# The query features on GpSimd, with wide products and a new order of steps

## The chip, the cores and the metric

The kernel runs on one core of a Trainium2 chip. The metric is the device time of one execution in microseconds. A core has five engines that run beside each other and wait for one another through semaphores: TensorE (PE, matrix products; PEld is its loading of weights), VectorE (DVE), ScalarE (ACT), GpSimd (POOL) and SyncE (SP), which here only issues transfers (DMA).

## The reference, cut to what matters

```python
def phi(x):                                  # x: [4, 4, 1088, 32]
    a = einsum('rd,bhsd->bhsr', S1, x)       # r = 8
    b = einsum('rd,bhsd->bhsr', S2, x)
    return einsum('bhsi,bhsj->bhsij', a, b)  # 64 features
kv  = einsum('bhsf,bhsd->bhfd', phi(k), v);  z = phi(k).sum(axis=2)
x   = (phi(q) @ kv) / (phi(q) @ z + 1e-6)    # 4352 tokens x 128
h   = x @ w_in                               # 4352 x 2048
P   = a0 + a1*h + a2*h**2 + a3*h**3
Q   = 1 + |b0|*|h| + |b1|*h**2
out = (P / (Q + 1e-6)) @ w_out
```

First comes a linear attention whose features are products of two sketches, then a layer with a rational function in the middle.

## The kernel before, in words

**Two halves that run at once.** The attention works by batch: `Keys` (lines 236 to 314) makes the sums over keys and values, `Queries` and `Spread` (lines 317 to 433) make x for blocks of queries and put it, transposed, into `xT`. The layer works by units: a unit is 4096 columns of (a stretch of features) x (a stretch of tokens), 17 in all, numbered 0 to 16 (lines 436 to 446). Units 1 to 14 have 512 tokens and 8 blocks of features; units 0, 15 and 16 have 256 tokens and all 16 blocks. A unit has two halves of 2048 columns; the second half of unit 16 is cut in two again (`QUARTER`).

**One unit.** PE makes h in four parts of 1024 columns (`hidden`, L455), ACT copies each into `hh` in bf16 (`evac`, L461). DVE makes u = |h| (L484), w = |b1| u + |b0| (L490) and w u (L495), for a whole unit at once or, for units in `SPLIT_A`, by halves. ACT makes r = 1/Q by a logarithm and an exponential (L546, L550), by halves. Then DVE makes s = h r (L554), and the third term in one of two ways. Normally p = a3 h + a2 comes from ACT or DVE (`P_ON_ACT` says which, half by half; L541, L536), m is g = h s (L558), x is g = g p (L569), and PE adds up r, s and g with three scaled copies of w_out (`gather`, L588). For the halves in `HORNER`, m is g = h p, then DVE adds a1 to g (step v, L564), x is g = g s, and PE adds up r and g alone: the s products fall away (L577). `WIDE_S`, `WIDE_M`, `WIDE_X` and `WIDE_P` name the units in which s, m, x or p is one instruction of 4096 columns instead of two of 2048 (`skip`, L518); for m and x both halves must be Horner or both not. r, s, g and p lie in rings (L497): four halves each for r, s and g, two for p.

**One block of queries.** The last ten blocks are `Spread`: PE makes the sketches (L409), ACT copies them to SBUF (L415), SP writes them to DRAM and reads them back spread out, as `a_all` and `b_all` (L420 to L428, one buffer each); then the features are their product (`features`, L432: 128 x 768 or 128 x 640 in f32), both factors in SBUF. PE multiplies the features with the sums of the keys (L365), ACT and DVE divide (L376, L380, L385), PE transposes (L391), ACT copies into `xT` (L398). The first three blocks (`Queries`) make their features from a factor in PSUM (L354, L357).

**The order.** `ORDER` (lines 21 to 57) is a list written out by hand: each entry is a step and its unit, block or batch, and every engine gets its instructions in that order. h0 to h3 and e0 to e3 are `hidden` and `evac`, u, w, y, ln, ex, pa (p on ACT), pd (p on DVE), s, m, v, x the steps above (0 and 1 behind a letter are the halves), G0 to G8 the parts of `gather`; qt, qs, qc, qf, qp, qd, qi, qx, qb, qk are the steps of a query block, qf its features, qp the product that reads them; kt to kk those of the keys; lk, lq, lv, lw, lx load; wo scales w_out; ba takes |b|; st writes out; tn:0 and tn:4 give PE 11 and 2 idle products (`TURNS`, L170) into an otherwise unused bank.

Of the kernel before, what the change touches and what calls it, by code (L numbers as in the profile page):

```python
# [26 lines left out]
ex0:0 u1:1 h2:2 qf:3 w1:1 qc:4 e1:2 qp:3 e2:2 s0:0 pa0:0 h3:2 y1:1 h0:2 qd:3 wo:5 e3:2 qi:3 m0:0 G0:0 e0:2 qx:3 G1:0
ln0:1 kt1:2 x0:0 qb:3 ks0:2 u1:2 qk:3 G2:0 ex0:1 lk:3 pd0:1 G3:0 w1:2 G4:0 pa1:1 kp1:1 y1:2 kc0:2 ln1:1 G5:0 qf:4 lv:2
qs:5 kf0:2 kk:1 ex1:1 qp:4 s0:1 ks1:2 qd:4 qc:5 qi:4 ln0:2 qt:7 G0:1 qx:4 m0:1 qb:4 G1:1 qk:4 s1:1 ex0:2 h3:3 x0:1
kc1:2 h2:3 m1:1 e3:3 kf1:2 h0:3 e2:3 kt1:3 ln1:2 s0:2 h1:3 st:0 m0:2 e0:3 qs:7 x1:1 e1:3 h2:4 ex1:2 u1:3 h3:4 pd1:2  # L30
pa0:2 w1:3 kp1:2 s1:2 e2:4 x0:2 e3:4 h0:4 lv:3 qf:5 pa0:3 y1:3 qp:5 qc:7 e0:4 h1:4 m1:2 qd:5 ln0:3 qi:5 qt:9 G2:1 qx:5
e1:4 x1:2 qb:5 G3:1 qk:5 u1:4 ex0:3 G4:1 m0:3 G5:1 pa1:3 G0:2 w1:4 h0:5 kt0:3 ln1:3 m1:3 h2:5 y1:4 kk:2 ex1:3 ks0:3
G1:2 e0:5 s1:3 G2:2 ln0:4 G3:2 h1:5 v0:3 ex0:4 qf:7 x0:3 G4:2 e2:5 qs:6 s0:4 qc:6 h3:5 e1:5 pd0:4 ln1:4 m0:4 h1:6 v1:3
e3:5 x0:4 pa1:4 h0:6 u1:5 qt:8 G5:2 e1:6 w1:5 ex1:4 h3:6 st:2 y1:5 e0:6 qp:7 e3:6 s1:4 G0:3 pa0:5 lq:3 G2:3 x1:3 qs:8
m1:4 h2:6 ln0:5 m0:5 G3:3 e2:6 x1:4 G5:3 ex0:5 qf:6 G0:4 u1:6 G1:4 qc:8 qd:7 ln1:5 qi:7 qp:6 w1:6 G2:4 qx:7 qd:6 pa0:6
qi:6 v0:5 qb:7 G3:4 qx:6 y1:6 qb:6 qk:7 G4:4 qk:6 ex1:5 h3:7 m0:6 pa1:5 G5:4 s1:5 h1:7 e3:7 st:4 h2:7 m1:5 e1:7 ln0:6
x0:5 h0:7 qt:10 x1:5 e2:7 G0:5 e0:7 qf:8 ks1:3 kc0:3 ex0:6 u1:7 qs:9 h1:8 v0:6 qc:9 w1:7 ln1:6 h3:8 s0:6 e1:8 pd1:6
qp:8 ex1:6 y1:7 h0:8 e3:8 s1:6 kc1:3 ln0:7 h2:8 x0:6 e0:8 m1:6 G2:5 qd:8 ex0:7 G3:5 qi:8 kf0:3 G4:5 kf1:3 G5:5 e2:8
qs:10 ln1:7 u1:8 kp1:3 qx:8 w1:8 ex1:7 qb:8 G0:6 qf:9 qk:8 y1:8 qc:10 h3:9 pa0:7 s0:7 h0:9 e3:9 s1:7 ln0:8 h2:9 qt:12
m0:7 e0:9 G0:7 x1:6 e2:9 h1:10 ex0:8 x0:7 qt:11 h1:9 u1:9 pa0:8 m1:7 G2:6 pd1:7 e1:9 G3:6 s0:8 e1:10 G4:6 u0:9 ln1:8  # L40
h3:10 w1:9 m0:8 qp:9 ex1:8 x1:7 h2:10 x0:8 qd:9 kk:3 e3:10 qi:9 w0:9 pa0:9 h0:10 qf:10 y0:9 qp:10 e2:10 y1:9 e0:10
G5:6 qx:9 qd:10 ln0:9 qi:10 qb:9 s1:8 G1:7 qx:10 G2:7 qk:9 u1:10 ex0:9 G3:7 m1:8 qb:10 G4:7 qk:10 s0:9 ln1:9 G5:7
qs:11 pd1:8 h1:11 w1:10 qc:11 ex1:9 x1:8 h0:11 e1:11 m0:9 pa1:9 h3:11 y1:10 e0:11 G0:8 s1:9 e3:11 h2:11 ln0:10 x0:9
h0:12 m1:9 e2:11 pd0:10 ex0:10 h1:12 u1:11 x1:9 e0:12 G1:8 w1:11 e1:12 G2:8 ln1:10 G3:8 s0:10 G4:8 y1:11 G5:8 ex1:10
qs:12 G0:9 m0:10 G1:9 ln0:11 h3:12 s1:10 ex0:11 x0:10 h2:12 qf:11 pa1:10 m1:10 G2:9 s0:11 G3:9 e3:12 G4:9 x1:10 qc:12
ln1:11 qp:11 pd0:11 m0:11 G5:9 qd:11 e2:12 G0:10 qi:11 x0:11 ex1:11 G1:10 u1:12 G2:10 pa1:11 qx:11 G3:10 w1:12 qb:11
G4:10 qk:11 s1:11 pa0:12 h1:13 y1:12 h3:13 e1:13 m1:11 ln0:12 h2:13 st:6 x1:11 ex0:12 G5:10 qf:12 G0:11 st:8 e3:13
qp:12 s0:12 e2:13 st:10 h0:13 ln1:12 m0:12 u1:13 h2:14 e0:13 x0:12 ex1:12 u0:13 h3:14 w1:13 w0:13 e2:14 y1:13 e3:14
h1:14 pa1:12 y0:13 h0:14 s1:12 qd:12 e1:14 qi:12 m1:12 G1:11 e0:14 qx:12 G2:11 ln1:13 u1:14 qb:12 G3:11 pd0:13 G4:11
ex1:13 w1:14 G5:11 x1:12 G0:12 qk:12 ln0:13 h0:15 s1:13 pd1:13 ex0:13 G1:12 y1:14 G2:12 e0:15 h2:15 s0:13 ln0:14 m1:13  # L50
h3:15 e2:15 m0:13 ex0:14 h1:15 x1:13 x0:13 e3:15 G3:12 s0:14 e1:15 h2:16 ln1:14 u1:15 G4:12 m0:14 ex1:14 G5:12 w1:15
# [17 lines left out]
@with_exitstack  # L69
def kernel(  # L70
    ctx: ExitStack,
# [164 lines left out]
    class Keys:  # L236
# [33 lines left out]
        def features(self, part):  # L270
            n = self.PARTS[part][1]
            k_p = self.k_p[part] = tmp.tile([128, 5, H, R, R], FP, name="k_p", bufs=3)
            nc.vector.tensor_mul(  # L273
                out=k_p[:, 0:n].rearrange("p t h i j -> p (t h) i j"),
                in0=self.ab[part][:, :, :, 0, :].rearrange("p t h r -> p (t h) r")[:, :, :, None]
                    .broadcast_to([128, n * H, R, R]),
                in1=self.sk[part][:, 0:n].rearrange("p t h r -> p (t h) r")[:, :, None, :]
                    .broadcast_to([128, n * H, R, R]))
# [123 lines left out]
    class Spread(Queries):  # L402
# [26 lines left out]

        def features(self):  # L430
            self.q_p = tmp.tile([128, 2, QW], FP, name="q_pT")
            nc.vector.tensor_mul(out=self.q_p[:, :, :self.n], in0=self.a[:, :2 * self.n].rearrange("p (c n) -> p c n", c=2),  # L432
                                 in1=self.bb[:, :2 * self.n].rearrange("p (c n) -> p c n", c=2))


# [52 lines left out]
    def d_w(i, c):
        t = mine(i, "w", mid, 2)
        nc.vector.tensor_scalar(out=t[:, c], in0=live[i]["u"][:, c], scalar1=ab1, scalar2=ab0, op0=AX.mult, op1=AX.add)  # L490

    @halves(SPLIT_A)
    def d_y(i, c):
        t = live[i]["w"]
        nc.vector.tensor_mul(out=t[:, c], in0=t[:, c], in1=live[i]["u"][:, c])  # L495
# [36 lines left out]

    @skip(WIDE_P, on_act)
    def d_p(i, h, hh):
        if not on_act(i, first(h)):
            nc.vector.tensor_scalar(out=part_of(i, "p", h), in0=hh, scalar1=a3, scalar2=a2, op0=AX.mult, op1=AX.add)  # L536
# [14 lines left out]

    @skip(WIDE_S)
    def d_s(i, h, hh):
        nc.vector.tensor_mul(out=part_of(i, "s", h), in0=hh, in1=part_of(i, "r", h))  # L554
# [163 lines left out]
```

## Time and profile before

| | |
|---|---|
| runs | 272.06, 272.32, 272.9 us, median 272.32 |
| span of the profiled execution | 270.8 us; its own time is given by no other number |
| PE, DVE, ACT, POOL busy | 257.7, 256.7, 248.8, 2.9 us |
| DVE instructions | 278 |
| DMA | 19.55 MB, mean 72 GB/s |

How to read it: a group of instructions has one line of the kernel, an engine, an operation, what it writes and reads with the shapes, and the count; then the busy time in us, the mean of one in ns, and the idle time ahead of them with what ended it. In a view by time a line begins with the start and the duration in us. Where instructions overlap, the busy time counts a moment once.

### The profile page before, as it was taken

Reading aid. Unit: us, or ns where it says so; the run is one execution under the profiler, and the core shown is the slowest. Engines: PE = TensorE matmul, PEld = TensorE weight load, DVE = VectorE, ACT = ScalarE, POOL = GpSimd, SP = SyncE. Lnnn points to the kernel's source line nnn. Section 1 sums busy time; section 2 is a strip of 40 time slices with the busy share of each in tenths; the row PEclk is TensorE's granted clock in tenths of the full one; section 3 lists DMA queues with packets and bytes.
Section 4 is the critical chain, followed back from the end, with each engine's and each line's share of the span. In section 5 each row is a group of like instructions: output and inputs, shape, how many; then the busy total and the mean of one; then the engine's idle time right before and its main releaser. Section 6 shows DMA issues by size and latency. Waiting matters only on the chain.

```text
span 270.8 us, 3732 instructions
## 1 busy us (share of the span) xinstructions
PE 257.7 (95%) x1382; PEld 147.5 (54%) x1397; DVE 256.7 (95%) x278; ACT 248.8 (92%) x224; POOL 2.9 (1%) x24
## 2 busy tenths in 40 slices
...
DVE  3777999999999999999999999999999999999994
ACT  1268999998999999999999999999999999999991
...
GB/s 167 265 323 151 156 38 136 117 90 96 76 106 34 12 118 100 77 75 33 97 6 123 7 0 3 119 11 0 15 97 73 43 0 0 2 39 1 0 2 79
DMA packets 30530, 19.55 MB, mean 72 GB/s; under 512 B 20400, under 2 KB 26672, under 8 KB 30512
## 3 DMA queue, kind: packets, MB, share of 16 engines
...
q8 instruction: 11, 0.18, 0.3%
...
## 4 chain that ended last, share of the span: by engine, by line
ACT 47%; PE 34%; issue 8%; DVE 5%; DMA 4%; SPq 0%; ACTq 0%; DVEq 0%
PE h_ps L455 16%; ACT ln L546 13%; ACT r L550 12%; ACT hh L461 12%; PE att_ps L588 10%; ACT p L541 7%; PE att_ps L365 3%; DMA v_sb<-in_v_dram 2%; PE att_ps L302 2%; DMA k_sb<-in_k_dram 2%; DVE g L558 2%; DVE s L554 1%; ACT xT L398 1%; PE att_ps L391 1%; PE att_ps L409 1%
## 5 line engine op out<-in xcount | busy, mean ns | idle before, releaser
L455 PE MATMUL h_ps<-xT,w_in_sb 128*128 128x512 f32 (+1 forms) x320 | 125.8, 537 | 2.8 <-ACT hh L461 1.9
L455 PEld LDWEIGHTS h_ps<-xT,w_in_sb 128*128 128x128 f32 x320 | 58.3, 190 | 55.2 <-issue 37.3
L461 ACT CAST hh<-h_ps 128x1024 bf16<-128x1024 f32 x68 | 67.5, 1027 | 3.5 <-PE h_ps L455 3.1
L588 PEld LDWEIGHTS <-w_out 128*128 128x128 bf16 x460 | 45.5, 100 | 45.9 <-issue 14.3
L546 ACT ACTIVATE ln<-w 128x2048 f32<-128x2048 bf16 (+1 forms) x35 | 66.0, 1887 | 0.7 <-DVE w L495 0.6
L550 ACT ACTIVATE r<-ln 128x2048 bf16<-128x2048 f32 (+1 forms) x35 | 65.8, 1880 | 0.6 <-PE att_ps L588 0.2
L541 ACT ACTIVATE p<-hh,a_sb 128x2048 bf16<-128x2048 bf16 (+1 forms) x23 | 46.7, 2035 | 0.1
L554 DVE TENSOR_TENSOR s<-hh,r 128x2048 bf16<-128x2048 bf16 (+2 forms) x33 | 41.0, 1246 | 0.2 <-ACT r L550 0.2
L495 DVE TENSOR_TENSOR w<-w,u 128x4096 bf16<-128x4096 bf16 (+2 forms) x22 | 39.4, 1798 | 0.1
L588 PE MATMUL att_ps<-g,w_out 128*128 128x512 bf16 (+1 forms) x154 | 34.8, 350 | 4.3 <-DVE g L569 3.9
L558 DVE TENSOR_TENSOR g<-hh,s 128x2048 bf16<-128x2048 bf16 (+1 forms) x30 | 35.2, 1175 | 0.0
L569 DVE TENSOR_TENSOR g<-g,p 128x2048 bf16<-128x2048 bf16 (+1 forms) x30 | 35.1, 1178 | 0.1
L588 PE MATMUL att_ps<-r,w_out 128*128 128x512 bf16 (+1 forms) x154 | 34.8, 353 | 0.3
L588 PE MATMUL att_ps<-s,w_out 128*128 128x512 bf16 (+1 forms) x137 | 29.3, 342 | 0.2
L490 DVE TENSOR_SCALAR w<-u,b_abs 128x4096 bf16<-128x4096 bf16 (+2 forms) x22 | 23.8, 1090 | 0.0
L484 DVE TENSOR_SCALAR u<-hh 128x4096 uint16<-128x4096 uint16 (+2 forms) x22 | 21.4, 976 | 1.6 <-ACT hh L461 1.5
L365 PEld LDWEIGHTS att_ps<-kvz,q_pT 128*128 128x128 f32 x144 | 17.7, 191 | 4.6 <-issue 2.0
L365 PE MATMUL att_ps<-kvz,q_pT 128*128 128x66 f32 x144 | 17.9, 273 | 0.1
L302 PEld LDWEIGHTS att_ps<-v_sb,k_p 128*64 128x64 f32 (+1 forms) x288 | 8.8, 138 | 1.9 <-DVE qT L325 0.8
L536 DVE TENSOR_SCALAR p<-hh,a_sb 128x2048 bf16<-128x2048 bf16 x12 | 9.7, 808 | 0.0
L302 PE MATMUL att_ps<-v_sb,k_p 128*64 128x64 f32 (+1 forms) x288 | 9.2, 223 | 0.5 <-DMA v_sb<-in_v_dram 0.5
L273 DVE TENSOR_TENSOR k_p<-att_ps,b_sk 128x1024 f32<-128x1024 f32 (+2 forms) x8 | 9.3, 1178 | 0.1
...
## 6 DMA issues: line engine op xcount, KB each, us to landing
...
```

The lines of the kernel that those rows point to most:

```text
L365: nc.tensor.matmul(self.nd[:, o:o + 2 * KW], lhsT=self.q_p[:, c, x:x + 128], rhs=kvz[self.b % 2][:, c, :], start=True, stop=True)
L455: nc.tensor.matmul(t[:, x * tl:(x + 1) * tl], lhsT=w_in_sb[:, f * 128:(f + 1) * 128], rhs=xT[:, x_at(t0):x_at(t0) + tl], start=True, stop= ...
L461: nc.scalar.copy(out=live[i]["hh"][:, part * PW:(part + 1) * PW], in_=live[i]["h", part])
L490: nc.vector.tensor_scalar(out=t[:, c], in0=live[i]["u"][:, c], scalar1=ab1, scalar2=ab0, op0=AX.mult, op1=AX.add)
L495: nc.vector.tensor_mul(out=t[:, c], in0=t[:, c], in1=live[i]["u"][:, c])
L541: nc.scalar.activation(out=part_of(i, "p", h), in_=hh, func=ACT.Identity, scale=a3, bias=a2)
L546: nc.scalar.activation(out=t, in_=live[i]["w"][:, span(h)], func=ACT.Ln, bias=1.0 + 1e-6)
L550: nc.scalar.activation(out=part_of(i, "r", h), in_=live[i]["ln"], func=ACT.Exp, scale=-1.0)
L554: nc.vector.tensor_mul(out=part_of(i, "s", h), in0=hh, in1=part_of(i, "r", h))
L558: nc.vector.tensor_mul(out=part_of(i, "g", h), in0=hh, in1=part_of(i, "p" if horner(i, first(h)) else "s", h))
L569: nc.vector.tensor_mul(out=g, in0=g, in1=part_of(i, "s" if horner(i, first(h)) else "p", h))
L588: nc.tensor.matmul(outs[t0][:, :tl], lhsT=w_sb[y][:, f0 + x, :], rhs=part_of(i, key, h)[:, c:c + tl], start=done[0] == 0, stop=done[0] == ...
```

## The change

The features of the ten `Spread` blocks are computed by GpSimd instead of DVE; the three earlier blocks stay on DVE. s, m and x of units 1 to 15 are one instruction each. Ten halves are Horner halves (both of units 0, 1, 2, 4 and 10) instead of five. Units 9 and 13 no longer split in u, w and y. p goes to DVE for 14 halves instead of 12, and seven units have a p of 4096 columns. `ORDER` is another list throughout; it names the same steps but for those that these settings add or drop. Of its lines only the few stand here that the text below speaks of.

```diff
 TURNS = (11, 0, 0, 0, 2, 0, 0, 0, 0)
 ORDER = """
-tn:4 tn:0 lw:1 lq:0 kt0:0 lw:0 kt1:0 lx:1 kt2:0 lx:0 ks1:0 kt3:0 ks0:0 lk:1 qt:0 ks2:0 kc0:0 kc1:0 kf0:0 kf1:0 qs:0
-kc2:0 qt:1 kf2:0 qc:0 kp0:0 ba:0 kp1:0 qf:0 kp2:0 wo:3 qs:1 kk:0 lv:1 qt:2 qp:0 qc:1 wo:1 qf:1 qs:2 qd:0 qi:0 qc:2
...
+kt1:0 ba:0 tn:0 kt3:0 ks1:0 kt0:0 kt2:0 kc1:0 kf1:0 ks0:0 qt:0 kc0:0 ks2:0 lq:0 kf0:0 kc2:0 qs:0 kp0:0 kp1:0 kf2:0
+kp2:0 qc:0 qt:1 qs:1 qf:0 kk:0 lx:1 qt:3 lw:0 qc:1 lk:1 qt:2 qp:0 qd:0 qi:0 qx:0 lw:1 qs:2 qb:0 qf:1 wo:4 qk:0 lq:1
...
+pa0:8 h2:10 qk:10 qf:11 w1:9 y1:9 h0:10 qc:12 qf:12 e2:10 ln0:9 pd1:8 s1:8 e0:10 G3:7 h1:11 ex0:9 h1:10 m1:8 e1:11
+e1:10 qp:11 qd:11 ln1:9 x1:8 G1:7 u1:10 G0:8 h0:11 w1:10 G2:7 G5:7 ex1:9 e0:11 h2:11 y1:10 s1:9 h3:11 qp:12 pa1:9 G5:8
...
+u3:16 G5:14 G0:15 w3:16 y3:16 m0:16 G1:16 ex2:16 x1:15 s2:16 ln3:16 G3:16 ex3:16 st:14 pa0:16 pa2:16 s3:16 G2:15 G4:16
+m2:16 tn:4 m3:16 pa3:16 x0:16 G7:16 G6:16 G5:15 st:15 G2:16 x2:16 x3:16 G5:16 G8:16 st:16
 """.split()
-P_ON_ACT = (1, 1, 0, 1, 1, 0, 1, 1, 0, 1, 1, 1, 1, 0, 1, 0, 1, 0, 1, 1, 0, 1, 0, 1, 1, 1, 0, 0, 1, 1, 0, 0, 1, 1)
-SPLIT_A = (0, 9, 13, 16)
+P_ON_ACT = (1, 1, 1, 1, 0, 0, 0, 1, 1, 0, 1, 0, 1, 1, 0, 0, 1, 0, 1, 1, 0, 0, 0, 0, 1, 0, 1, 1, 0, 1, 1, 1, 1, 1)
+SPLIT_A = (0, 16)
-WIDE_S = (3, 5)
-WIDE_M = (5,)
-WIDE_X = (5, 14)
-WIDE_P = (2,)
-HORNER = (6, 7, 10, 12, 29)
+WIDE_S = (1, 2, 3, 4, 5, 6, 7, 8, 9, 10, 11, 12, 13, 14, 15)
+WIDE_M = (1, 2, 3, 4, 5, 6, 7, 8, 9, 10, 11, 12, 13, 14, 15)
+WIDE_X = (1, 2, 3, 4, 5, 6, 7, 8, 9, 10, 11, 12, 13, 14, 15)
+WIDE_P = (2, 7, 9, 10, 11, 13, 15)
+HORNER = (0, 1, 2, 3, 4, 5, 8, 9, 20, 21)
         def features(self):
             self.q_p = tmp.tile([128, 2, QW], FP, name="q_pT")
-            nc.vector.tensor_mul(out=self.q_p[:, :, :self.n], in0=self.a[:, :2 * self.n].rearrange("p (c n) -> p c n", c=2),
+            nc.gpsimd.tensor_mul(out=self.q_p[:, :, :self.n], in0=self.a[:, :2 * self.n].rearrange("p (c n) -> p c n", c=2),
                                  in1=self.bb[:, :2 * self.n].rearrange("p (c n) -> p c n", c=2))
```

More of the change, by code (lines that the diff above doesn't have):

```diff
@@ L27 @@
[L27 to L51, printed above, removed]
@@ new lines @@
+kc1:2 pa0:1 kt0:3 e0:2 h3:2 w1:1 kp1:1 qi:3 qx:3 qs:7 m1:1 ex0:0 qf:5 kk:1 y1:1 e3:2 h1:2 qp:4 h2:2 e1:2 s0:0 G5:0
+qd:4 qi:4 qc:7 ln0:1 qx:4 e2:2 x0:0 kf1:2 qb:3 G0:0 ex0:1 qf:7 qp:5 qd:5 qk:3 qb:4 qk:4 pd1:2 lv:2 ln1:1 G2:0 ex1:1
+qs:6 qt:9 u1:2 G3:0 qi:5 qc:6 v1:1 qf:6 w1:2 h2:3 h0:3 qx:5 e2:3 h3:3 y1:2 e0:3 ln0:2 qt:8 qs:8 qb:5 s1:1 h1:3 e3:3
+qc:8 h0:4 m1:2 v0:1 G3:1 e1:3 h2:4 x1:1 G0:1 qk:5 u1:3 v0:2 ex0:2 G2:1 ln1:2 e2:4 v1:2 qp:6 ex1:2 qf:8 h1:4 e0:4 pa1:3
+w1:3 y1:3 qd:6 G5:1 h3:4 e1:4 e3:4 ln0:3 st:0 s1:2 ex0:3 ln1:3 lq:3 qs:9 qi:6 qx:6 u1:4 kp1:2 x1:2 G0:2 h1:5 qt:10
@@ new lines @@
+ks1:3 kk:2 h2:5 w1:4 G5:2 qs:10 qc:9 G2:2 kc1:3 y1:4 kf1:3 qp:7 ex1:3 pd0:3 qf:9 e1:5 ln0:4 h0:5 qb:6 qc:10 qd:7 e2:5
+e0:5 ex0:4 h3:5 qk:6 e3:5 h2:6 ln1:4 s1:3 m1:3 qp:8 qi:7 h1:6 qd:8 G3:2 qx:7 e2:6 x1:3 pa0:4 pd1:4 qi:8 qb:7 qx:8 u1:5
+ex1:4 h3:6 G0:3 ks0:3 w1:5 G2:3 e1:6 qk:7 y1:5 G1:3 e3:6 kc0:3 h0:6 ln0:5 m1:4 h0:7 s1:4 G3:3 pd1:5 e0:6 u1:6 ex0:5
+G4:3 st:2 v1:4 ln1:5 e0:7 v0:4 kf0:3 qb:8 lv:3 ex1:5 h2:7 w1:6 qk:8 y1:6 G0:4 h1:7 e2:7 G5:3 h3:7 e1:7 s1:5 ln0:6 e3:7
+G3:4 qf:10 pa0:5 kp1:3 h1:8 kk:3 h0:8 m1:5 ex0:6 x1:4 G0:5 x1:5 u1:7 G2:4 qt:11 w1:7 qp:9 ln1:6 e0:8 h3:8 y1:7 ex1:6
@@ new lines @@
+qs:11 G5:5 pa0:6 e1:8 e3:8 pa1:6 G5:4 h2:8 G2:5 qc:11 s1:6 m1:6 G4:5 qd:9 ln0:7 e2:8 st:4 h3:9 G3:5 qi:9 ex0:7 qx:9
+G4:6 e3:9 x1:6 u1:8 ln1:7 h2:9 e2:9 ex1:7 w1:8 G3:6 y1:8 pd1:7 ln0:8 h1:9 G1:5 G0:6 qp:10 h0:9 G1:6 qd:10 qt:12 s1:7
+qi:10 ex0:8 e1:9 qx:10 qb:10 m1:7 G2:6 G5:6 e0:9 h3:10 ln1:8 u1:9 ex1:8 st:6 qb:9 G0:7 G4:7 e3:10 qk:9 qs:12 x1:7
+pa0:8 h2:10 qk:10 qf:11 w1:9 y1:9 h0:10 qc:12 qf:12 e2:10 ln0:9 pd1:8 s1:8 e0:10 G3:7 h1:11 ex0:9 h1:10 m1:8 e1:11
+e1:10 qp:11 qd:11 ln1:9 x1:8 G1:7 u1:10 G0:8 h0:11 w1:10 G2:7 G5:7 ex1:9 e0:11 h2:11 y1:10 s1:9 h3:11 qp:12 pa1:9 G5:8
```

21 lines of the change are left out of this document (13 added, 8 removed).

## The prediction

> **What bounds the kernel now.** I read the totals of the page first, then its slices in time, then the busy time in chosen stretches, then the groups of instructions by shape, and last the instructions in order of time.
>
> ```profile
> span 270.8 us, 3732 instructions
> PE 257.7 (95%) x1382; PEld 147.5 (54%) x1397; DVE 256.7 (95%) x278; ACT 248.8 (92%) x224; POOL 2.9 (1%) x24
> DVE  3777999999999999999999999999999999999994
> ACT  1268999998999999999999999999999999999991
> ```
>
> Three engines are busy for 92 to 95% of the span and GpSimd (POOL) for 1%. From the fifth slice to the last but one VectorE (DVE) never falls under nine tenths. The stretches say it more sharply (busy us of PE, PEld, DVE, ACT, POOL, then the clock):
>
> ```profile
> 180.00:200.00 20.00, 19.95 (x92) 9.75 (x92) 20.00 (x20) 19.90 (x16) 0.00 (x0) 1.00 0.13 38
> 250.00:260.00 10.00, 7.62 (x46) 5.07 (x46) 10.00 (x11) 9.34 (x6) 0.00 (x0) 0.83 0.01 2
> ```
>
> In the middle DVE is busy for 20.00 of 20 us, in the tail for 10.00 of 10 while PE waits. So DVE is the first bound: what its queue gains or loses there, the end gains or loses. PE and ACT stand right behind it, so a gain of DVE alone is soon cut short, while a loss of DVE counts in full.
>
> The times: 270.8 us is the span of the profiled execution, the only length that the profile gives for it; the median of the three runs is 272.32, which leaves 1.5 us around the span. I work in differences and add them to 272.3.
>
> **The change part by part.** First how long an instruction holds its queue:
>
> ```profile
> 182.47 2.29 DVE L495 TENSOR_TENSOR w<-w,u 128x4096 bf16<-128x4096 bf16 x1
> 184.67 1.22 DVE L558 TENSOR_TENSOR g<-hh,s 128x2048 bf16<-128x2048 bf16 x1
> ...
> 188.08 0.95 DVE L432 TENSOR_TENSOR q_pT<-a_all,b_all 128x768 f32<-128x768 f32 x1
> 188.83 2.08 ACT L541 ACTIVATE p<-hh,a_sb 128x2048 bf16<-128x2048 bf16 x1
> 188.94 1.22 DVE L558 TENSOR_TENSOR g<-hh,s 128x2048 bf16<-128x2048 bf16 x1
> 190.08 1.22 DVE L554 TENSOR_TENSOR s<-hh,r 128x2048 bf16<-128x2048 bf16 x1
> 190.82 0.99 ACT L461 CAST hh<-h_ps 128x1024 bf16<-128x1024 f32 x1
> ```
>
> The columns are start, duration, engine. Each instruction starts 0.08 to 0.09 us before the one ahead has ended: a 2048-wide product costs DVE 1.14 us (188.94 to 190.08), a 4096-wide one 2.20 (182.47 to 184.67), a query product 0.86 (188.08 to 188.94), a p on ACT 1.99. From each duration below I take off 0.08 on DVE and 0.09 on ACT.
>
> ```profile
> L554 DVE TENSOR_TENSOR s<-hh,r 128x2048 bf16<-128x2048 bf16 x29 | 35.1, 1213 | 0.0
> L558 DVE TENSOR_TENSOR g<-hh,s 128x2048 bf16<-128x2048 bf16 x28 | 33.8, 1210 | 0.0
> L569 DVE TENSOR_TENSOR g<-g,p 128x2048 bf16<-128x2048 bf16 x28 | 33.7, 1214 | 0.0
> L554 DVE TENSOR_TENSOR s<-hh,r 128x4096 bf16<-128x4096 bf16 x2 | 4.6, 2292 | 0.2 <-ACT r L550 0.2
> L490 DVE TENSOR_SCALAR w<-u,b_abs 128x4096 bf16<-128x4096 bf16 x13 | 17.3, 1333 | 0.0
> L490 DVE TENSOR_SCALAR w<-u,b_abs 128x2048 bf16<-128x2048 bf16 x7 | 5.5, 795 | 0.0
> L536 DVE TENSOR_SCALAR p<-hh,a_sb 128x2048 bf16<-128x2048 bf16 x12 | 9.7, 808 | 0.0
> L564 DVE TENSOR_SCALAR g<-g,a_sb 128x2048 bf16<-128x2048 bf16 x5 | 3.7, 734 | 0.0
> L432 DVE TENSOR_TENSOR q_pT<-a_all,b_all 128x768 f32<-128x768 f32 x6 | 5.7, 952 | 0.0
> L432 DVE TENSOR_TENSOR q_pT<-a_all,b_all 128x640 f32<-128x640 f32 x4 | 3.3, 817 | 0.0
> ```
>
> *Wide s, m, x.* Units 1 to 15 get one instruction each for s, m and x. Before, two s are wide and no m or x (half pairs that differ in Horner stay apart), so 13 + 15 + 15 = 43 pairs merge, each for 2 × 1.14 − 2.20 = 0.08 us: **−3.4 us**. It is this little because a pair already overlaps.
>
> *Units 9 and 13 no longer split in u, w, y.* w saves 2 × 0.72 − 1.25 = 0.18, y the 0.08 of a product, u I put between: 0.4 a unit, **−0.8 us**.
>
> *Ten Horner halves for five.* Five more additions v at 0.73 − 0.08 = 0.65: **+3.3 us**. The Horner m and x are products of the same shape, so no change there.
>
> *p.* After, 14 halves are on DVE for 12, eight of them as four wide ones. A wide p isn't in the trace; the wide w (1333 ns, same type and width, also two scalars) is the nearest row: 6 × 0.72 + 4 × 1.25 − 12 × 0.72 = **+0.7 us**. Together these four come to −0.2 us on DVE: they cancel.
>
> *The ten query products leave DVE:* 6 × 0.86 + 4 × 0.73 = **−8.1 us**. So DVE's own list falls by 8.3 us, if GpSimd costs it nothing.
>
> *ACT* loses two halves of p, and three pairs become wide:
>
> ```profile
> L541 ACT ACTIVATE p<-hh,a_sb 128x2048 bf16<-128x2048 bf16 x21 | 44.3, 2112 | 0.1
> L541 ACT ACTIVATE p<-hh,a_sb 128x1024 bf16<-128x1024 bf16 x2 | 2.4, 1226 | 0.0
> ```
>
> 1024 more columns cost 0.886 us, so a wide p is 2.112 + 1.772 − 0.09 = 3.79 for 3.98. ACT: −2 × 1.99 − 3 × 0.19 = **−4.6 us**.
>
> *PE.* A Horner half has no s matmuls. After, unit 0 (256 tokens) and units 1, 2, 4, 10 are Horner in both halves: 16 matmuls of 256 columns and 32 of 512 are gone, before 20 of 512.
>
> ```profile
> 248.68 1.03 PE L588 MATMUL att_ps<-s,w_out 128*128 128x512 bf16 x4
> 249.54 1.03 PE L588 MATMUL att_ps<-g,w_out 128*128 128x512 bf16 x4
> ```
>
> Four of 512 take 0.86 us from start to start, 0.215 each; a 256 I put at half. PE: −12 × 0.215 − 16 × 0.108 = **−4.3 us**.
>
> *What GpSimd's products cost.* Its nearest rows:
>
> ```profile
> L212 POOL TENSOR_TENSOR SAB<-sT,mask 128x128 f32<-128x128 f32 x2 | 0.8, 398 | 0.0
> L174 POOL MEMSET mask<- 128x4 f32 x1 | 0.1, 101 | 0.3 <-POOLq L702 0.3
> ```
>
> A memset of 4 elements takes 101 ns, which I take as the fixed part; the 128-element product then has (398 − 101) / 128 = 2.32 ns per element. 768 elements: 1.78 us and the fixed part; 640: 1.49. The ten: 6 × 1.78 + 4 × 1.49 = 16.6 us of reading and multiplying, twice DVE's 8.1. GpSimd itself has room for it.
>
> The question is what DVE does meanwhile, and no row of before shows it. GpSimd's last work stands here beside DVE's next:
>
> ```profile
> 4.00 0.76 POOL L212 TENSOR_TENSOR SAB<-sT,mask 128x128 f32<-128x128 f32 x2
> 5.07 1.62 DVE L254 STREAM_TRANSPOSE kT<-k_sb 128x256 f32<-128x256 f32 x4 [1.46 <-DMA k_sb<-in_k_dram]
> ```
>
> DVE idles while GpSimd multiplies, so the two never read SBUF at once. The ends: DVE loses **nothing**, or it stands still for the whole **16.6 us**. No reason lets DVE run faster beside GpSimd, so nothing lies below zero. I take the far end less a tenth. Most of DVE's list is products with both operands in SBUF, GpSimd's own kind, back to back. u, w, v and p have one operand, but 2048 more columns cost them 0.54 us (1333 − 795) against 1.08 for a product (2292 − 1213): they read as many words in a time as a product's two operands do, so I count them with the products. GpSimd finds no opening in that list. What could run beside it are DVE's slower reads, transposes and instructions with an operand in PSUM:
>
> ```profile
> L385 DVE TENSOR_TENSOR x_tok<-att_ps,rec 128x384 f32<-128x384 f32 x10 | 5.4, 544 | 0.0
> L597 DVE STREAM_TRANSPOSE out_sb<-att_ps 128x512 f32<-128x512 f32 x7 | 5.0, 709 | 0.0
> L325 DVE STREAM_TRANSPOSE qT<-q_sb 128x384 f32<-128x384 f32 x6 | 3.3, 556 | 0.0
> L254 DVE STREAM_TRANSPOSE kT<-k_sb 128x864 f32<-128x864 f32 x3 | 3.2, 1061 | 0.0
> ```
>
> ```profile
> L273 DVE TENSOR_TENSOR k_p<-att_ps,b_sk 128x1024 f32<-128x1024 f32 (+2 forms) x8 | 9.3, 1178 | 0.1
> ```
>
> They make 26.2 of 256.7 us, a tenth. So DVE stands for 0.9 × 16.6 = **15.0 us**, and its balance is −8.3 + 15.0 = **+6.7 us**. (The last row is the page's, three shapes together.)
>
> The Trainium skill speaks against this change in "SBUF — State Buffer", section "Who interferes with whom": a DVE instruction with two SBUF inputs and a GpSimd instruction that reads SBUF want the same second read port, and whoever comes second waits for the whole of the first. By that page the sum is the one with +6.7; without it the sum ends at −8.3; no run here shows it yet. The Trainium skill's "GPSIMD Engine Reference", section "Elementwise — side-by-side cycle accounting", gives 4497 ns against DVE's 2293 for 2048 elements; by that ratio the ten would be an estimated 17 us, close to what the rows give.
>
> *The new waits.* GpSimd's product waits for the a_all and b_all transfers, as DVE's did; nothing is queued behind it on GpSimd. What waits for it: PE's products L365 and all that PE has behind them, and SP's next load of a_all, of which there is one buffer. In the new order the last blocks have at least 0.72 + 2.20 + 2.20 us of DVE work (pd1:8, s1:8, m1:8) between qf:12 and qp:12, which covers 1.9 us of GpSimd and one DVE instruction ahead of it. I cost this at nothing; without that cover, each block adds up to 2 us to PE.
>
> *The order.* Steps of start and tail move: two idle matmuls (tn:4) go from the head to the tail, |b| is taken earlier on ACT, the loads of w_out, w_in and q come in another sequence on SP. In the tail DVE is full (10.00 of 10 us) while the clock is 0.83, so a warmer PE buys nothing there; at the head the chain hangs on transfers. Wide pieces let the last gathers start up to 1.1 us later. I put the order at 0 with 2 us to either side.
>
> Sum: 272.3 + 6.7 = **279.0 us**.
>
> **The rivals.** *Side by side.* GpSimd's products take nothing from DVE. For it: no row shows a conflict, GpSimd is empty, and all three full engines get shorter. Then PE is the bound: 272.3 − 4.3 = 268.0, or 264.0 if DVE alone decides; I put it at **267**. It decides as soon as DVE loses less than 8.3 of the 16.6 us, half of GpSimd's time; above that the change is slower.
>
> *DVE goes first.* GpSimd gets in only at DVE's openings (that tenth of its list). DVE then keeps most of its 8.3 us, but the features come late, PE stands before L365, and DVE runs dry behind it. At 0.8 us for each of ten blocks the gain is gone: **272**, between 269 and 275. Against it: DVE's instructions start before the one ahead ends, but each still ends.
>
> *The order is worse in itself.* Wide products hold back the gathers of each first half by 1.1 us. Only on top of one of the others; it is in the 2 us.
>
> **How the numbers follow.** The forecast (they take turns) 0.58, from 275 (half of the price's doubt) to 284 (all 16.6 and 2 for the order); side by side 0.32, from 263 to 269; DVE first 0.10. About 0.3% is what the measurement of this kernel can tell from no change (its runs lie between 272.06 and 272.9). Faster: nearly all of side by side and a third of DVE first, 0.34; same 0.04; slower 0.62. The range must reach into side by side: from 265 to 283 it leaves out some 0.08 at the bottom and 0.07 at the top. The forecast's own range is 275 to 284.
>
> **What would show it.** GpSimd should show ten products of 1.6 to 1.9 us or longer. If they take turns, the DVE product beside each will last up to 1.8 us longer than its mean, DVE's busy total will rise towards 263 and the mean of wide s above 2292 ns. If side by side, DVE's durations stay and its total is near 248, with PE at 253 and gaps on DVE. If DVE goes first, GpSimd's products look long or start late, and PE waits before L365. Wrong would also be: ACT not near 244, or a stop in the start of more than 2 us.

## The result and the profile after

The changed kernel takes **284.75 us** (median of four runs, 284.45 to 286.62) where the kernel before takes 272.34 on the same chip: a ratio of 1.0462 with the interval [1.0436, 1.0487], so 12.4 us slower. (Ratios, here and below, are of the fast runs alone: a run that took over 1.5% longer than the fastest of its kernel is left out of them.) The direction is the forecast's, and so is the way in which GpSimd holds DVE. The size is not: 279.0 was forecast, 5.75 us less, the time lies 1.75 us above the range, and what the sum took for the bound was not the bound.

The totals of the changed kernel, two engines in 40 slices, and the shares of its chain of waits:

```profile
span 282.6 us, 3640 instructions
PE 258.9 (92%) x1369; PEld 147.4 (52%) x1369; DVE 263.4 (93%) x222; ACT 246.1 (87%) x219; POOL 26.5 (9%) x34
...
DVE  3679698999999999999999999999999999999993
ACT  1269989676999998789999999999998999999991
...
DVE 73%; DMA 10%; issue 9%; SPq 3%; ACT 2%; PE 1%; DVEq 0%; ACTq 0%
```

DVE has 56 instructions fewer than before and is busy 6.7 us longer, to a total of 263.4 us, which is the total forecast. But it also stands idle for 19.2 us of the span (282.6 − 263.4) where that was 14.1 (270.8 − 256.7). ACT, which had no slice under eight tenths between the fifth and the last, now has several: it waits. The same chain line of the kernel before, which the prediction does not use, reads otherwise:

```profile
ACT 47%; PE 34%; issue 8%; DVE 5%; DMA 4%; SPq 0%; ACTq 0%; DVEq 0%
```

Before, the end hung on ACT and PE, and DVE held 5% of the chain. After, DVE holds 73%. GpSimd's new work by shape (busy, mean ns of one):

```profile
L429 POOL TENSOR_TENSOR q_pT<-a_all,b_all 128x768 f32<-128x768 f32 x6 | 14.4, 2405 | 84.7 <-DMA b_all<-sk_d 84.7
L429 POOL TENSOR_TENSOR q_pT<-a_all,b_all 128x640 f32<-128x640 f32 x4 | 9.1, 2271 | 67.4 <-DMA b_all<-sk_d 67.4
```

Then one such product and DVE's instructions around it, by time (start, duration):

```profile
64.78 1.97 POOL L429 TENSOR_TENSOR q_pT<-a_all,b_all 128x768 f32<-128x768 f32 x1 [8.89 <-DMA b_all<-sk_d]
...
65.45 3.43 DVE L492 TENSOR_TENSOR w<-w,u 128x4096 bf16<-128x4096 bf16 x1
...
69.31 2.24 DVE L551 TENSOR_TENSOR s<-hh,r 128x4096 bf16<-128x4096 bf16 x1
```

The DVE product that meets GpSimd's lasts 3.43 us, the one after it 2.24. Going through all ten in the trace and taking off each DVE instruction's undisturbed mean, DVE is held for 0, 1.44, 1.60, 1.13, 1.36, 0.80, 1.22, 1.51, 1.20 and 1.12 us: 11.4 in all. No other DVE instruction is stretched. Five of the ten (0, 1.13, 0.80, 1.22 and 1.20) ran partly beside a transpose, a reciprocal or a product with an operand in PSUM, and these kept their length. Here a transpose of an operand in SBUF, 0.51 us long (0.49 in the mean before), passes beside GpSimd, and only the product behind it is held:

```profile
155.14 2.41 POOL L429 TENSOR_TENSOR q_pT<-a_all,b_all 128x768 f32<-128x768 f32 x1 [42.72 <-DMA b_all<-sk_d]
155.79 0.51 DVE L322 STREAM_TRANSPOSE qT<-q_sb 128x320 f32<-128x320 f32 x1
156.22 3.48 DVE L551 TENSOR_TENSOR s<-hh,r 128x4096 bf16<-128x4096 bf16 x1
```

In the first 31 us DVE waits longer for keys, 3.8 us in all and 2.2 at the longest, where it was 1.7 and 1.5 before. The prediction named a stop of more than 2 us in the start as a sign against it:

```profile
DVE kT L251 <- DMA k_sb<-in_k_dram: 3.8, 3, 2.2
```

### The profile page after: what moved, and what is told of

Its sections match the earlier page's. It is cut to its first block, busy times and chain, and to the rows that moved or that the text cites. A ratio compares the mean times of both kernels' runs of the same rounds, so it can differ in the third digit from the quotient of the medians.

```text
span 282.6 us, 3640 instructions
## 1 busy us (share of the span) xinstructions
PE 258.9 (92%) x1369; PEld 147.4 (52%) x1369; DVE 263.4 (93%) x222; ACT 246.1 (87%) x219; POOL 26.5 (9%) x34
## 4 chain that ended last, share of the span: by engine, by line
DVE 73%; DMA 10%; issue 9%; SPq 3%; ACT 2%; PE 1%; DVEq 0%; ACTq 0%
DVE s L551 14%; DVE g L566 11%; DVE g L555 11%; DVE w L492 10%; DVE w L487 8%; DVE u L481 7%; DMA q_sb<-in_q_dram 4%; DMA w_out_sb_f<-in_moe_w_out_dram 4%; DVE p L533 3%; DVE out_sb L594 2%; DVE x_tok L382 2%; DVE g L561 2%; DVE k_p L270 2%; DMA sk_d<-sk_sb 2%; DVE qT L322 1%
## 5 line engine op out<-in xcount | busy, mean ns | idle before, releaser
L492 DVE TENSOR_TENSOR w<-w,u 128x4096 bf16<-128x4096 bf16 (+2 forms) x20 | 42.0, 2102 | 0.5
L538 ACT ACTIVATE p<-hh,a_sb 128x2048 bf16<-128x2048 bf16 (+2 forms) x18 | 40.9, 2285 | 1.6 <-DVE g L566 1.5
L551 DVE TENSOR_TENSOR s<-hh,r 128x4096 bf16<-128x4096 bf16 (+2 forms) x20 | 42.0, 2099 | 0.0
L429 POOL TENSOR_TENSOR q_pT<-a_all,b_all 128x768 f32<-128x768 f32 (+1 forms) x10 | 23.5, 2351 | 152.1 <-DMA b_all<-sk_d 152.1
L566 DVE TENSOR_TENSOR g<-g,p 128x4096 bf16<-128x4096 bf16 (+2 forms) x14 | 28.8, 2064 | 0.2
L555 DVE TENSOR_TENSOR g<-hh,s 128x4096 bf16<-128x4096 bf16 (+2 forms) x14 | 27.7, 1982 | 0.7
L585 PE MATMUL att_ps<-s,w_out 128*128 128x512 bf16 (+1 forms) x112 | 24.9, 353 | 2.7 <-DVE s L551 2.7
L566 DVE TENSOR_TENSOR g<-g,s 128x4096 bf16<-128x4096 bf16 (+1 forms) x6 | 11.6, 1930 | 0.1
L555 DVE TENSOR_TENSOR g<-hh,p 128x4096 bf16<-128x4096 bf16 (+1 forms) x6 | 11.6, 1926 | 0.0
L270 DVE TENSOR_TENSOR k_p<-att_ps,b_sk 128x1280 f32<-128x1280 f32 (+2 forms) x8 | 9.3, 1168 | 1.3 <-ACT b_sk L265 1.3
```

The costliest lines, as they stand in the source:

```text
L538: nc.scalar.activation(out=part_of(i, "p", h), in_=hh, func=ACT.Identity, scale=a3, bias=a2)
L555: nc.vector.tensor_mul(out=part_of(i, "g", h), in0=hh, in1=part_of(i, "p" if horner(i, first(h)) else "s", h))
L566: nc.vector.tensor_mul(out=g, in0=g, in1=part_of(i, "s" if horner(i, first(h)) else "p", h))
L585: nc.tensor.matmul(outs[t0][:, :tl], lhsT=w_sb[y][:, f0 + x, :], rhs=part_of(i, key, h)[:, c:c + tl], start=done[0] == 0, stop=done[0] == ...
```

## The experiments

Times are medians; ratios are to the kernel before on the same chip, with 95% intervals.

### The two halves of the change, apart

**The changed kernel with the features back on DVE.**

```diff
-            nc.gpsimd.tensor_mul(out=self.q_p[:, :, :self.n], ...
+            nc.vector.tensor_mul(out=self.q_p[:, :, :self.n], ...
```

> The changed kernel with one word undone: VectorE multiplies the query features again, all else (order, wide products, Horner halves) stays. Theory 1 (they take turns, and half of the loss lies elsewhere): in the changed kernel VectorE's instructions beside GpSimd's ten products lasted 11.4 us longer than their like; VectorE's own ten products cost 8.1 us. So undoing it saves 3.3 us: 281.5 us. Rival 2 (all of the loss is GpSimd's, by turns and by late features together): 272 us or less. Rival 3 (GpSimd costs nothing, the order does it): 284.7 us.

Measured: 310.97 us, 1.1418 [1.1375, 1.1461]. Every theory missed. The view of waits names a cause that none had (waited for: us in total, times, longest):

```profile
DVE q_pT L429 <- DMA b_all<-sk_d: 29.8, 6, 7.2
```

The new list puts qf where the transfer has not landed. On GpSimd that cost nobody, as nothing is queued behind it there; on DVE all the rest stands behind it. So this run does not price GpSimd, it shows that the order and the engine belong together.

**The kernel before with the features on GpSimd,** the same edit the other way round, and nothing else.

> The kernel before with that one word alone: GpSimd multiplies the ten features, nothing else changes. Theory 1: VectorE is held 1.1 to 1.2 us for each, 11.4 in all, and is rid of 8.1: 275.6 us, VectorE's stretched instructions visible beside each product. Forecast as it was made, 15.0 us held: 279. Rival 2: 284 or more. Rival 3 (side by side): 265 to 268.

Measured: 279.67 us, 1.0263 [1.024, 1.0287]. Its totals:

```profile
span 277.8 us, 3764 instructions
PE 260.9 (94%) x1397; PEld 148.4 (53%) x1397; DVE 260.5 (94%) x268; ACT 249.6 (90%) x224; POOL 28.4 (10%) x34
```

Moving the ten products alone costs 7.2 us, in the old order too. DVE is busy 3.8 us longer although it has ten instructions fewer; by the same count as above it is held for 11.6 us. One of the ten cost it nothing:

```profile
138.42 2.07 POOL L432 TENSOR_TENSOR q_pT<-a_all,b_all 128x640 f32<-128x640 f32 x1 [13.67 <-DMA b_all<-sk_d]
139.00 0.22 DVE L380 RECIPROCAL rec<-den 128x12 f32<-128x12 f32 x1
139.14 2.55 DVE L273 TENSOR_TENSOR k_p<-att_ps,b_sk 128x1024 f32<-128x1024 f32 x2
```

Beside it stood products with an operand in PSUM, and they kept their length (1.16 and 1.47 us; these shapes have 1.20 and 1.48 in the mean of the kernel before).

**s, m, x as halves again, features on DVE.** The lists of wide units empty, and each wide step written as two side by side.

```diff
-WIDE_S = (1, 2, 3, 4, 5, 6, 7, 8, 9, 10, 11, 12, 13, 14, 15)
+WIDE_S = ()
...
-... h3:3 y1:2 e0:3 ln0:2 qt:8 qs:8 qb:5 s1:1 h1:3 e3:3
+... h3:3 y1:2 e0:3 ln0:2 qt:8 qs:8 qb:5 s0:1 s1:1 h1:3 e3:3
```

> As the first, and s, m, x of units 1 to 15 are two instructions of 2048 again, set one behind the other where the wide one stood. Theory 1: 45 pairs cost 0.08 us each more (3.6 us), but 12 products no longer read what stands right ahead of them (0.14 us each, 1.7 us less) and the gathers of first halves may start 1.1 us earlier: about 282 to 283, near the first. Rival (wide products themselves are the loss, as they hold back the gathers): 277 or less.

Measured: 312.38 us, 1.1454 [1.1432, 1.1477], within the interval of the first run. The same wait for b_all covers everything, so it decides nothing on the width. The run with halves further below does.

### The disputed cost by itself

A small program in eight stages, with nothing in it but the instructions in dispute.

> The disputed cost by itself; this kernel computes nothing of the reference and writes zeros. Eight stages: VectorE's bf16 products of 4096 that don't read each other; the same, each reading the one ahead; GpSimd's f32 products of 768 alone; beside VectorE's products; beside VectorE's one-operand instructions; beside VectorE's f32 products with one operand in PSUM; then GpSimd's fills of 2048 f32, which read nothing, beside VectorE's products and beside its one-operand instructions. Theory 1 (they take turns at reading SBUF): a GpSimd product alone 1.6 to 1.9 us; beside products and one-operand instructions each of the five holds VectorE for 1.4 to 1.7 us; beside PSUM products for nothing; fills hold products for nothing. A product that reads the one ahead starts 0.12 to 0.19 us later than one that doesn't. Rival (they share by word, each slowed a little): no single VectorE instruction is long, all are somewhat longer. Rival (they take turns at everything): PSUM products and fills hold VectorE as well.

First DVE alone, by time: seven products that do not read each other, then eight of which each reads the one ahead.

```profile
14.52 15.50 DVE L50 TENSOR_TENSOR z<-h,r 128x4096 bf16<-128x4096 bf16 x7
32.79 18.58 DVE L65 TENSOR_TENSOR z<-z,r 128x4096 bf16<-128x4096 bf16 x8
```

With 2.28 us for the last of a row, the first come every (15.50 − 2.28) / 6 = 2.20 us, the second every (18.58 − 2.28) / 7 = 2.33: a product that reads its neighbour starts **0.13 us later**. Then single instructions by shape (busy, mean ns), cut out of the stages by narrow windows: GpSimd alone; DVE's product and GpSimd's beside each other; a one-operand instruction undisturbed and beside GpSimd's product; products from PSUM and GpSimd's beside them.

```profile
L47 POOL TENSOR_TENSOR fo<-fa,fb 128x768 f32<-128x768 f32 x1 | 1.8, 1799 | 0.1
...
L50 DVE TENSOR_TENSOR z<-h,r 128x4096 bf16<-128x4096 bf16 x1 | 3.9, 3883 | 0.0
L47 POOL TENSOR_TENSOR fo<-fa,fb 128x768 f32<-128x768 f32 x1 | 3.8, 3846 | 0.0
...
L53 DVE TENSOR_SCALAR z<-h 128x4096 bf16<-128x4096 bf16 x2 | 2.3, 1214 | 0.0
L53 DVE TENSOR_SCALAR z<-h 128x4096 bf16<-128x4096 bf16 x1 | 2.8, 2819 | 0.0
...
L56 DVE TENSOR_TENSOR z<-p,f 128x512 bf16<-128x512 f32 x15 | 9.0, 678 | 0.0
L47 POOL TENSOR_TENSOR fo<-fa,fb 128x768 f32<-128x768 f32 x5 | 8.9, 1809 | 0.1
```

GpSimd's 768 columns take 1.80 us alone (1.78 and the fixed part were forecast). Beside a DVE product both take 3.9: first one multiplies and the other stands, then they change. DVE loses 3.88 − 2.28 = **1.60 us** for each, beside a one-operand instruction 2.82 − 1.21 = 1.61. Beside products from PSUM, GpSimd keeps its 1.81 and DVE its 0.68, the mean of all 24 of that stage. So "they take turns" holds for DVE's products with both operands in SBUF and for its one-operand instructions here, and not for products with one operand in PSUM. It is what the Trainium skill says in "SBUF — State Buffer", section "Who interferes with whom"; that section has no price for this case, and here it is up to 1.6 us for 0.86 us of DVE work saved.

### What else the change did to DVE's list

In the changed kernel's trace u, w, y and then s, m, x often stand right behind each other, by time:

```profile
202.96 1.22 DVE L481 TENSOR_SCALAR u<-hh 128x4096 uint16<-128x4096 uint16 x1
204.22 1.35 DVE L487 TENSOR_SCALAR w<-u,b_abs 128x4096 bf16<-128x4096 bf16 x1
205.60 2.29 DVE L492 TENSOR_TENSOR w<-w,u 128x4096 bf16<-128x4096 bf16 x1
207.81 0.75 DVE L561 TENSOR_SCALAR g<-g,a_sb 128x2048 bf16<-128x2048 bf16 x1
```

w reads u and starts 0.04 us behind its end, y reads w and starts 0.03 behind it; v belongs to another unit and starts 0.08 ahead of the end. By the order there are 51 such dependent neighbours, before 15. By the traces 53 start less than 0.06 us ahead of the end of what they read, before 11.

**Parting them,** in the kernel with the features on DVE: 43 of the 51 places get a step of another unit between. A piece of its order:

```diff
-... lq:2 w0:0 s1:0 x1:0 ...
+... lq:2 s1:0 w0:0 x1:0 ...
```

> As the first, and the order is changed in VectorE's steps alone: where an instruction reads what the one right ahead of it writes (51 places), another is put between them (8 places are left). Theory 1: in the changed kernel such a neighbour starts 0.03 to 0.10 us behind the end of the one ahead, others 0.085 before it; 43 places at 0.13 are 5.6 us: about 276. Rival: the time isn't VectorE's to give, other waits fill it, or the later results make ScalarE wait: 280 to 282.

Measured: 323.84 us, 1.1786 [1.1747, 1.1824], by the ratios (1.1786 − 1.1418) 10 us slower than without. Whatever the neighbours cost, moving steps a few places costs more in this list. It is no price for them.

**The features on DVE, where GpSimd began them.** Each qf moved to the place in the order at which GpSimd really started in the changed kernel; two buffers for a_all and b_all, and the idle products 256 wide and twice as many.

```diff
-    PB, AB = 1, 1
+    PB, AB = 1, 2
...
-... wo:0 qs:4 qf:3 wo:1 ...
+... wo:0 qs:4 wo:1 ...
...
-... v1:0 lv:1 kt1:2 ...
+... v1:0 lv:1 qf:3 kt1:2 ...
```

> The changed kernel with the features on VectorE, this time put in VectorE's list where the changed kernel's GpSimd began them, since in the list as it stands VectorE waits up to 7 us for their factors. So that the list allows it, a_all and b_all have two buffers, and the idle products are 256 wide and twice as many. Theory 1: VectorE is rid of 11.4 us held and gets 8.1 us of products: 281.5; with the waits that follow from the holding gone too (3.5 us, by what GpSimd alone cost the kernel before: 6.9 in all) 278. Rival 2 (all the loss is GpSimd's): 272 or less. Rival 3 (the order is the loss): 284 or more.

Measured: 282.32 us, 1.0374 [1.0315, 1.0433]. Even with no turns the new order stays 10 us behind. How much of that is the placing, which was found for GpSimd's times, or the other two edits is not shown.

**Halves, with GpSimd.** The changed kernel with s, m and x as halves, as in the third run.

> The changed kernel, its features on GpSimd as they are, with s, m and x of units 1 to 15 as two instructions of 2048 each, side by side in the list. Theory 1: 45 pairs cost 0.08 us more each (3.6), 13 neighbours that read what stands right ahead fall away (1.8): 286 to 287. Rival (wide products are part of the loss, holding back gathers or holding VectorE from GpSimd for long): 282 or less.

Measured: 286.91 us, 1.0504 [1.0473, 1.0536]. The changed kernel on the same chip has 1.0497 [1.0478, 1.0516] (further below), so the two can't be told apart: the wide instructions are not the loss, and a gain by them is not shown either.

**Loads sooner.**

```diff
-... lw:0 qc:1 ... qx:0 lw:1 qs:2 ... kt1:1 qc:3 ... qd:1 lk:2 qi:1 ...
+... lw:0 lw:1 qc:1 ... qx:0 qs:2 ... kt1:1 lk:2 qc:3 ... qd:1 qi:1 ...
```

> The changed kernel with two loads issued sooner: the second half of w_out right behind the first, and the keys of batch 2 ahead of the transfers of the fourth query block. Theory 1: VectorE stood still for 2.2 us for these keys, 0.8 for w_out and about as long again behind them; PE and ScalarE have room, so 282 to 283. Rival: the time is lost later anyway, as another transfer comes later instead: 284 to 285.

Measured: 289.01 us, 1.0621 [1.0565, 1.0676]: slower, also than the changed kernel's 1.0497. DVE's longest wait for keys is 1.5 us again, but in its place:

```profile
DVE qT L322 <- DMA q_sb<-in_q_dram: 6.1, 1, 6.1
```

**The head of before.** The first 69 steps of the old order, without tn:4, then the rest of the new.

```diff
-kt1:0 ba:0 tn:0 kt3:0 ks1:0 kt0:0 kt2:0 kc1:0 ...
+tn:0 lw:1 lq:0 kt0:0 lw:0 kt1:0 lx:1 kt2:0 ...
```

> The changed kernel with the head of the order of before: the first 69 steps (to the load of the keys of batch 2, without tn:4) in the old order, all others in the new. Theory (of the 11.8 us of span that were lost, 3.3 are GpSimd's turns, 4.1 neighbours that read what stands right ahead, 3.6 VectorE's stops in the first 45 us, 0.8 the tail): 281 us. Rival (the stops of the head are made up for or come back later): 284 to 287.

Measured: 288.68 us (285.99 to 290.18), 1.0551 [1.0495, 1.0606].

**The changed kernel again,** on that chip, without an edit.

> The changed kernel itself on this chip, as the measure for the others: 284.5 to 286.6 as before. If VectorE's stop in the head (its transpose of queries that waits for PE) is 2.7 us here and not 1.3, then this stop varies with the transfers and not with the edits of the last runs.

Measured: 286.31 us, 1.0497 [1.0478, 1.0516]. So the head of before brings no gain; the two intervals overlap.

**Both, the head of before and the features on DVE.**

> The kernel with the features on VectorE in fitting places, with the head of the order of before: what is left of the change is wide products, Horner halves, p and the order behind the head. Theory: 282.3 less 3.6, 278 to 279, so some 6 us stay that are neither GpSimd's nor the head's. Rival (head and GpSimd were all): 273 or less.

Measured: 288.42 us, 1.0575 [1.0531, 1.0619]. Theory and rival missed: DVE again waits for b_all (7.4 us), as the head moved the times for which qf had been placed.

**Two blocks on GpSimd, in the kernel before,** chosen where its trace showed DVE on PSUM operands.

```diff
+            (nc.gpsimd if (self.b, self.c0) in ((0, 768), (2, 768)) else nc.vector).tensor_mul(...
```

> The kernel before, with GpSimd multiplying the features of two of the ten blocks only: those two (the first and the seventh of the ten) beside which VectorE lost 0.4 us and nothing, since it worked on products from PSUM there. Theory 1 (turns only where both read SBUF): VectorE saves 2 x 0.73 and loses 0.4: 271.7 us for 272.7, if the products fall in the same places. Rival (every product on GpSimd costs its turn): 273.5 to 274.

Measured: 272.73 us against 272.8, 0.9998 [0.9989, 1.0007]. By time:

```profile
34.82 1.54 POOL L432 TENSOR_TENSOR q_pT<-a_all,b_all 128x640 f32<-128x640 f32 x1 [30.06 <-DMA b_all<-sk_d]
34.93 2.50 DVE L569 TENSOR_TENSOR g<-g,p 128x2048 bf16<-128x2048 bf16 x1
134.38 2.56 DVE L273 TENSOR_TENSOR k_p<-att_ps,b_sk 128x1024 f32<-128x1024 f32 x2
134.53 1.55 POOL L432 TENSOR_TENSOR q_pT<-a_all,b_all 128x640 f32<-128x640 f32 x1 [98.17 <-DVE rec L380]
```

One fell beside k_p and was free, the other met a product and held it (2.50 for 1.21). Together they are worth nothing that can be measured.

### What was still open: which term of the sum was wrong

**Dependent neighbours in the kernel before.** u, w and y of thirteen units put right behind each other: 44 such places instead of 15.

```diff
-... u1:1 h2:2 ... qf:3 w1:1 qc:4 ... h3:2 y1:1 h0:2 ...
+... u1:1 w1:1 y1:1 h2:2 ... qf:3 qc:4 ... h3:2 h0:2 ...
```

> The kernel before with its own settings and its features on VectorE, but in units 1 to 15 without 9 and 13 the three steps u, w, y stand right behind each other in the list, each reading what the one ahead of it writes: 44 such neighbours instead of 15. Theory (such a neighbour costs 0.13 us, as alone on the chip): 29 x 0.13 = 3.7 us, 276.4. Rival (the logarithm gets its input sooner and pays for it, or the gap is hidden): 272 to 273.5. Rival 2 (the order is so tight that any move costs more than its gap): 279 or more.

Measured: 295.64 us, 1.0835 [1.0817, 1.0853]. The 29 new places account for some 3 us of it by the starts in the trace. Nearly all the rest is DVE standing idle, 35.3 us of the span (294.7 − 259.4) where it was 14.1, for instance:

```profile
DVE u L486 <- ACT hh L463: 8.1, 6, 2.9
```

**The changed kernel without the turns.** GpSimd fills the features with ones and multiplies only 8 of the columns.

```diff
-            nc.gpsimd.tensor_mul(out=self.q_p[:, :, :self.n], in0=..., in1=...)
+            nc.gpsimd.memset(self.q_p[:, :, :self.n], 1.0)
+            nc.gpsimd.tensor_mul(out=self.q_p[:, :, :4], in0=...[:, :, :4], in1=...[:, :, :4])
```

> The changed kernel with the turns taken away and all else left: GpSimd fills the features with ones, which reads nothing, and multiplies only 8 of the 768 or 640 columns, so that it still waits for both factors; 760 columns of the features are not computed. Theory (the turns cost the 11.4 us that VectorE was held, and little else): 273 to 276. Rival (the new order loses its time elsewhere, and a free VectorE waits instead): 280 or more.

Measured: 275.45 us (273.79 to 278.81), 1.0085 [1.0056, 1.0114], as expected. Everything of the change is in it but GpSimd's long reads; the fills are new. Three of DVE's groups by shape, first of the changed kernel, then of this one (busy, mean ns), and the totals of this one:

```profile
L492 DVE TENSOR_TENSOR w<-w,u 128x4096 bf16<-128x4096 bf16 x15 | 37.0, 2468 | 0.4
L551 DVE TENSOR_TENSOR s<-hh,r 128x4096 bf16<-128x4096 bf16 x15 | 35.4, 2358 | 0.0
L481 DVE TENSOR_SCALAR u<-hh 128x4096 uint16<-128x4096 uint16 x15 | 20.4, 1360 | 0.0
```

```profile
L493 DVE TENSOR_TENSOR w<-w,u 128x4096 bf16<-128x4096 bf16 x15 | 34.3, 2289 | 0.4
L552 DVE TENSOR_TENSOR s<-hh,r 128x4096 bf16<-128x4096 bf16 x15 | 34.1, 2276 | 0.0
L482 DVE TENSOR_SCALAR u<-hh 128x4096 uint16<-128x4096 uint16 x15 | 18.2, 1214 | 0.0
```

```profile
PE 254.4 (93%) x1355; PEld 145.2 (53%) x1369; DVE 254.2 (93%) x222; ACT 245.7 (90%) x219; POOL 21.1 (8%) x44
```

The same 222 instructions are busy 9.2 us less (263.4 − 254.2), and u, which reads only hh, is shorter just as the products are. The fills still hold DVE: four one-operand instructions that met one (two v, a p and a w) last 0.5 to 0.6 us longer, 2.2 us together, so that the 9.2 us are 11.4 − 2.2. In the group of v it shows (734 ns before):

```profile
L562 DVE TENSOR_SCALAR g<-g,a_sb 128x2048 bf16<-128x2048 bf16 x10 | 8.3, 843 | 0.1
```

The difference of the ratios, 1.0462 − 1.0085, puts these 9.2 us at 10.3 us of the end; against the 1.0497 of the changed kernel when it was run again (above) it is 11.2.

**The same in the kernel before.** Here the edit takes the ten products off DVE and puts next to no reading in their place: the credit of the prediction, alone.

> The same in the kernel before: what GpSimd would give there if it took no turns. By VectorE's list 272.7 less 8.1: 264.6; if PE is the bound, 268 or more; if the order stays the bound, 272. The distance between this run and the one of the changed kernel is what its other edits cost without GpSimd: 5 us if GpSimd's part is the same in both, 0 to 2 as the prediction had it, 8 or more if the new order hides part of GpSimd's turns.

Measured: 272.85 us, 1.0004 [0.9995, 1.0013]. Its totals and its chain:

```profile
PE 258.0 (95%) x1382; PEld 147.7 (54%) x1397; DVE 249.9 (92%) x268; ACT 248.9 (92%) x224; POOL 21.1 (8%) x44
...
PE 46%; ACT 33%; DVE 7%; issue 7%; DMA 5%; SPq 1%; DVEq 0%; ACTq 0%
```

DVE is busy 6.8 us less than before (a fill holds it once, for 0.45 us), and the time is the same to a tenth of a per cent. The middle shows why. The same stretch of both kernels (busy us of PE, PEld, DVE, ACT, POOL), before first:

```profile
140.00:180.00 40.00, 39.05 (x137) 18.44 (x138) 39.62 (x41) 39.95 (x37) 0.00 (x0) 1.00 0.15 45
```

```profile
140.00:180.00 40.00, 39.05 (x137) 18.38 (x137) 38.32 (x39) 39.95 (x37) 2.86 (x3) 1.00 0.15 45
```

DVE falls from 39.62 to 38.32 of 40, ACT stays at 39.95 and PE at 39.05. DVE got openings and ACT had none to follow with; DVE now stands for ACT instead:

```profile
DVE rec L380 <- ACT den L376: 4.2, 3, 1.9
...
DVE u L485 <- ACT hh L462: 2.3, 4, 0.9
```

## Why the prediction was right in direction and wrong in size

**What bounds the kernel: wrong, and this decided the size.** "So DVE is the first bound" rested on DVE's 20.00 of 20 us in one stretch and 10.00 of 10 in the tail. In the first of them ACT had 19.90 and PE 19.95, so a full DVE told nothing apart. The chain, with 5% for DVE, did. The text even said that a gain of DVE alone is cut short, and then its sum did not follow it.

**The ten query products leave DVE, −8.1 us: the step that failed.** Taken alone it is worth 0.1 us or less (1.0004, interval [0.9995, 1.0013]): what DVE gains there it spends waiting for ACT.

**DVE stands still for 15.0 us: right in kind, too large.** They take turns, up to 1.60 us for a DVE instruction. DVE was held for 11.4 us: none of the ten held it for more than 1.60 us, one for 0.80 and one not at all, where the forecast had 1.5 for the mean. The tenth that was taken off for transposes and PSUM operands was too little: half of the ten met such an instruction. At the end 10.3 us show in the changed kernel (1.0462 − 1.0085), and that leaves out what the fills hold; in the old order it is 7.1 (1.0263 − 1.0004) of 11.6, where DVE had some slack.

That the kernel before with GpSimd came out at +7.2, close to the +6.9 that −8.1 and +15.0 make, is therefore chance: the credit was 8 too large and the price in the end 8 too large as well. DVE's busy total came out as forecast, +6.7 us, by luck of the same kind: it is 11.4 held (15.0 forecast), −6.8 for the ten products by the run without reading (−8.1 forecast), and what is left, some 2 us, for the other edits (−0.2 forecast).

**The other edits: −0.2 and an order of 0 ± 2 were forecast; without the turns they cost 2.2 us** (1.0085 − 1.0004; the interval of the first is [1.0056, 1.0114]), at the edge of that bound, and what the fills cost, which hold DVE for 2.2 us, is in it. Of the sizes put in, DVE's wide p came out (1.34 us for 1.333), ACT's wide p nearly (3.80 us long for 3.88); that wide s, m and x gain 3.4 us is not shown. Two losses had no term. Dependent neighbours, 51 for 15, start later: at the 0.13 us of the small program that is an estimated 5 us over the list. And ACT's logarithm waits for y, where the order puts it close, in the changed kernel and in the kernel before:

```profile
ACT ln L543 <- DVE w L492: 6.8, 6, 2.4
```

```profile
ACT ln L546 <- DVE w L495: 0.6, 1, 0.6
```

How the loss divides among neighbours, head and tail is **not settled**: each of the runs that moved steps (neighbours parted or made, loads sooner, the old head) brought new waits larger than what it was to measure.

**Which term is to blame depends on the way through the runs.** By the runs without reading, the loss of 4.62% is 0.1 us for the products that leave, 2.2 for the other edits and 10.3 for the turns; these differences make up the whole by construction, so their sum confirms nothing. With the features on DVE in the new order the kernel is at +10.2 (1.0374): by this way the other edits cost 10.2, with the reservations of that run, and GpSimd adds 2.4, or 3.4 against the changed kernel run again, near the −8.1 + 11.4 = +3.3 of the prediction's own step with the measured hold. Both ways say the same: the ten products are worth nothing on DVE in the old order and some 7.9 us (1.0374 − 1.0085) in the new one, where the chain gives DVE 73%, if the placing and the two other edits cost nothing. The terms do not add up on one list, as the sum had it. Relative to the kernel before the credit could not be booked; what it is that makes DVE the last in the new order is not separated.

**The rivals.** "Side by side" is refuted by the small program. It would not have given 267 either: with no turns the changed kernel takes 275.45. "DVE goes first" is refuted by the alternation, 3.88 and 3.85 us. Features that come late were costed at nothing: PE waits for GpSimd's product in one block of the changed kernel, for 1.9 us, and PE holds 1% of the chain. A slower PE is no cause that shows either: between 45 and 100 us the granted clock is 0.94 (1.00 before), but DVE is busy for 54.66 of these 55 us.

**PE and ACT.** ACT is busy 246.1 (near 244 was forecast). PE in the run without turns is busy 254.4 (253 was forecast for it); that both are shorter brought nothing, as DVE holds 69% of that run's chain.

No version here beats the kernel before; the nearest, two blocks on GpSimd, equals it.
